# Three output projections one group later in the third stage of a long-convolution kernel, and the ring loads behind them

## The chip, the cores and the metric

The kernel runs on one core of a Trainium2 chip. The metric is the device time of one execution in microseconds. Before the change three runs took 935.6, 933.1 and 936.11 us (median 935.6). One execution was also profiled.

Five engines run side by side, each through its own queue in order: TensorE (PE for its matmuls, PEld for its weight loads), VectorE (DVE), ScalarE (ACT), GpSimd (POOL) and SyncE (SP, which here only starts transfers). ScalarE's queue starts some transfers too.

## The reference, cut to what matters

Eight batches of 6400 tokens with 128 channels, in float32. A causal convolution over the whole length, one filter for each channel, then a gated block:

```
x = irfft(rfft(x, 2*S) * rfft(h, 2*S))[:, :S]        # S = 6400, per channel
gate_pre[t] = sum over k < 5 of conv_w[k] * x[t-4+k]  # five taps, per channel
gate = sigmoid(gate_pre)
out = (gate * (x @ w_val)) @ w_out                    # two 128x128 projections
```

## The kernel before, in words

**The convolution in four stages.** The 6400 tokens are a grid of 100 by 64 (`N1`, `N2`). A first stage (`Forward.half`, table `r1_sb`) transforms along the 100, a second (`s2_mm`, table `m2` from memory) along the 64 for each frequency; its result is multiplied with the filter's spectrum, which the kernel computed at its start and keeps in memory (`hd`). A third stage (`s3_quads`, table `r3_sb`) and a fourth (`Chunk.s4`, table `m4_sb`) transform back. The second stage and the spectrum products run in 13 blocks (`kb`), each with 512 KB of table and 512 KB of spectrum.

**A batch in two parts.** The first part is 16 groups (`for g in range(NS)`, line 663). Group `g` does eight channels of batch b's third stage and eight channels of batch b+1's first stage, and some gated-block work of batch b-1. The second part interleaves the fourth stage of batch b with the second stage of batch b+1. The fourth stage gives the convolution's result in 13 chunks, named by their first column: 60 (four columns) and 0, 5, ..., 55 (five columns each, a tile of 128 channels by 500 tokens). Chunks 10 to 55 of a batch are not finished there: most of their gated block is left to the 16 groups of the next batch (the outputs of 55 and 60 follow in its second part). So in batch 0 no chunk is pending in the groups, and in batch 7 there is no first stage of a next batch.

**A chunk's steps.** `taps` adds the five-tap sum into gate tiles (ScalarE, VectorE, and `add` on GpSimd). `project` is the value projection (two matmuls on TensorE into one PSUM bank), `sigm` the sigmoid on ScalarE, and `gate` multiplies the value in PSUM into the gate tile on VectorE, after which that bank is free. `output` is the output projection (two matmuls into another bank); `store` copies it to SBUF on ScalarE, after which that bank is free, and starts its transfer to memory on SP's queue. Two tables say in which group a chunk takes which step: `VALUE` (line 48) for `project`, `sigm` and `gate`, `OUTPUT` (line 49) for `output`; `store` follows one group after `output` (lines 657 to 661). Within a group the pending chunks come in the order 60, 35, 40, 45, 50, 55, 10, 25, 15, 20, 30, each with all its steps of that group. "Value 30" and "output 20" below are chunk 30's value projection and chunk 20's output projection.

**A group's program.** TensorE: 64 matmul records of the third stage into a pair of PSUM banks, 32 of the first stage into two single banks, then the chunks' projections (four records each). ScalarE: a copy of half of the pair ("keep") and two small copies ("ends"), then, where the group has one, the start of a ring load (`ahead`), then two copies of the first stage's banks, then chunk work. VectorE: two additions that read the pair and set it free ("joins"), then taps and gates of the chunks. GpSimd: the first stage's sums for the group after next (each set free for a load of x on SP's queue), then `add`.

**PSUM.** Two pairs of banks serve the third stage, and four single banks (the pool `ps1`, line 632) everything else: the first stage's two halves, value and output projections. Which single bank a tile gets is fixed when the program is laid out, from the order in which banks come free in the plan; a tile whose bank is still in use waits on the chip for the instruction that frees it.

**The order.** Every instruction is kept in the order in which the program traces it on its engine (`keep_in_program_order`, line 122). Engines wait for each other only where data or a buffer makes them. All instructions therefore carry line 122 in the profile; they are told apart by tile names.

**The ring.** One SBUF tile of seven slots (`ring`) is shared. In the second part slots 0, 1, 2 hold blocks of the table `m2` and slots 3 to 6 spectrum blocks. In the groups the same space holds pending chunks: the gate tiles of chunks 10 to 30 lie in slots 0 to 2 (`held_c`, line 163), their convolution results in slots 2 to 4 (`held_y`, line 164); `store` writes the finished output over that result. As chunks finish, the first blocks of the second part are loaded back in halves of 256 KB, on ScalarE's queue. The table `AHEAD` (line 52) says in which group: `(0, kb, half)` loads a half block of `m2`, which needs the gate tiles there to have been read by `output`; `(1, kb, half)` loads a half block of the spectrum, which needs the stored outputs there to have left for memory.

The lines of a group's pending work:

```
            steps[t] += [c.project]
            steps[t if a in OUTPUT else NS - 1] += [c.sigm, c.gate]
            if a in OUTPUT:
                steps[OUTPUT[a]] += [c.output]
                steps[OUTPUT[a] + 1] += [c.store]
```

Of the kernel before, what the change touches and what calls it, by code (L numbers as in the profile page):

```python
# [45 lines left out]
M2_AT = (14, 19, 24, 27, 29)  # L46
KR = 117
VALUE = {10: 0, 15: 1, 20: 2, 25: 4, 30: 5, 35: 6, 40: 8, 45: 10, 50: 12, 55: 14}
OUTPUT = {10: 2, 15: 3, 20: 4, 25: 6, 30: 7, 35: 8, 40: 9, 45: 11, 50: 13}
ORDER = (60, 0, 35, 40, 45, 50, 55, 5, 10, 25, 15, 20, 30)  # L50
KEEP = {0: 1, 5: 3, 10: 1, 15: 2, 20: 3}
AHEAD = {
    2: (1, 0, 0), 3: (1, 0, 1), 4: (0, 0, 0), 5: (0, 0, 1), 7: (1, 1, 0), 8: (0, 1, 0),
    9: (0, 1, 1), 10: (0, 2, 0), 11: (0, 2, 1), 12: (1, 1, 1), 13: (1, 2, 0), 14: (1, 2, 1),
}


# [77 lines left out]
def longconv_moe(ctx: ExitStack, tc: tile.TileContext, x, h, r1, m2, r3, m4, w64, out):  # L135
# [504 lines left out]
    for b in range(B):  # L640
# [4 lines left out]
        for c in pend:  # L645
# [11 lines left out]
# [5 lines that stand above are left out]
        pend = [c for c in pend if c.ch[0] in (HEAD[0], HEAD[0] - CH)]  # L662
# [143 lines left out]
```

## Time and profile before

| | |
|---|---|
| time of the profiled execution | 933.86 us |
| its span, first to last instruction | 932.0 us |
| mean granted TensorE clock | 0.985 |
| TensorE matmul busy | 855.5 us (92%) |
| VectorE busy | 744.5 us (80%) |
| GpSimd busy | 560.4 us (60%) |
| ScalarE busy | 515.7 us (55%) |
| HBM read and written | 135.90 and 32.77 MB, 181 GB/s |

In the rows below a number ahead is the start in us from the span's first instruction, then the length, engine, line, operation, `out<-in` by tile names, shape and count; neighbours of one kind are merged into one row. In brackets stands how long the engine was idle before the row and which engine's work, on which tile, ended that. Names to know: `r_sb,gy` are the third stage's matmuls, `r_sb,sd` the first stage's, `ring,w_sb` the projections of chunks 10 to 30 and `yl,w_sb` or `gl,w_sb` those of later chunks; `dt<-pt,ring` on VectorE are the joins, `ring<-pt,ring` with 500 columns the gates, `SCALAR_TENSOR_TENSOR` the taps; on ScalarE `ring<-pt` with 512 columns is the keep, `gy<-pt` the first stage's copies, `ring<-pt` with 500 columns a store. Ends of matmuls are modelled, so a busy TensorE need not be one at its peak.

### The profile page before, as it was taken

To read this page: it belongs to the slowest core of one execution; us is meant where nothing else is said; L and a number is where in the kernel's file an instruction comes from. 1 tells how busy PE (TensorE), PEld (TensorE's weight loads), DVE (VectorE), ACT (ScalarE), POOL (GpSimd) and SP (SyncE) were. 2 spreads that over 40 slices of the span, in tenths; PEclk is the share of its full clock that TensorE was granted. 3 is DMA by queue.
4 is the path that set the end of the run, shared out by engine and by line. 5 is a ranking of instruction groups with operands and counts; after the bars stand their busy time and mean duration, and the time that the engine had idled before them with its cause. 6 is when DMAs were issued, how large, how long until landed. Compare 5 with 4: busy or idle time off the path is not lost. (4 is left out here: it accounts for less than half of the span.)

```text
span 932.0 us, 48248 instructions
## 1 busy us (share of the span) xinstructions
PE 855.5 (92%) x21360; PEld 683.5 (73%) x21360; DVE 744.5 (80%) x1057; ACT 515.7 (55%) x1238; POOL 560.4 (60%) x570
## 2 busy tenths in 40 slices
PE   6799668999999999999999999999999989999897
PEld 6699668965699558976689567985689657984563
DVE  5456657888887978888797978888897887978786
ACT  6532452277624874177623875167723785258776
POOL 0046644786477864877477855877558763765333
PEclk9899889999999999999999999999999999999999
DMA  7786647926594456925585465925586364921112
GB/s 241 228 294 225 188 140 238 339 67 185 171 312 154 147 175 204 317 70 172 164 298 180 127 189 171 329 87 167 176 275 223 107 181 159 326 78 48 67 57 99
DMA packets 77847, 171.80 MB, mean 184 GB/s; under 512 B 15246, under 2 KB 28558, under 8 KB 77638
## 3 DMA queue, kind: packets, MB, share of 16 engines
q1 hardware_dynamic: 65542, 146.68, 47.0%
q10 hardware_dynamic: 12096, 22.03, 8.2%
q8 instruction: 168, 2.75, 1.3%
q14 instruction: 41, 0.34, 0.1%
HBM read 135.90 MB, written 32.77 MB: 181 GB/s over the span
## 5 line engine op out<-in xcount | busy, mean ns | idle before, releaser
L122 POOL TENSOR_TENSOR gy<-gy,ring 128x512 f32<-128x512 f32 (+1 forms) x182 | 220.4, 1240 | 103.9 <-DVE ring L122 52.6
L122 PEld LDWEIGHTS pt<-r_sb,gy 64*64 64x64 f32 x8192 | 143.2, 138 | 108.1 <-issue 73.9
L122 PEld LDWEIGHTS pt<-m_sb,dt 128*64 128x64 f32 x4096 | 184.8, 136 | 24.0 <-issue 10.6
L122 DVE TENSOR_TENSOR dt<-pt,ring 128x496 f32<-128x496 f32 x256 | 159.6, 665 | 47.2 <-ACT dt L122 45.9
L122 PE MATMUL pt<-m_sb,dt 128*64 128x100 f32 x4096 | 191.4, 248 | 4.3 <-DVE ring L122 2.9
L122 PE MATMUL pt<-gy,ring 128*64 128x128 f32 x3008 | 187.6, 278 | 8.2 <-PE pt L122 3.1
L122 ACT COPY ring<-pt 128x512 f32<-128x512 f32 (+2 forms) x216 | 128.2, 601 | 116.6 <-PE pt L122 48.8
L122 POOL TENSOR_TENSOR sd<-x 128x256 f32<-128x256 f32 x224 | 179.6, 831 | 17.9 <-issue 13.3
L122 PEld LDWEIGHTS pt<-gy,ring 128*64 128x64 f32 x3008 | 174.7, 135 | 20.3 <-PE pt L122 8.0
L122 PE MATMUL pt<-r_sb,gy 64*64 64x64 f32 x8192 | 162.6, 226 | 19.9 <-issue 14.2
L122 PE MATMUL pt<-r_sb,sd 50*64 50x100 f32 x4608 | 141.0, 260 | 25.7 <-issue 18.6
L122 DVE TENSOR_TENSOR gy<-pt,ring 128x1024 f32<-128x1024 f32 (+1 forms) x99 | 117.0, 1182 | 55.5 <-PE pt L122 53.7
L122 PEld LDWEIGHTS pt<-r_sb,sd 50*64 50x64 f32 x4608 | 119.0, 142 | 31.8 <-issue 21.9
L122 DVE TENSOR_TENSOR ring<-pt,ring 128x1024 f32<-128x1024 f32 (+2 forms) x131 | 134.6, 1027 | 7.0
L122 ACT COPY gy<-pt 128x400 f32<-128x400 f32 x256 | 113.5, 503 | 30.8 <-PE pt L122 24.9
L122 ACT COPY yl<-pt 128x500 f32<-128x500 f32 (+1 forms) x89 | 51.2, 575 | 125.9 <-PE pt L122 125.8
L122 POOL TENSOR_TENSOR gl<-gl,p 128x500 f32<-128x500 f32 (+1 forms) x46 | 54.1, 1177 | 101.9 <-DVE gl L122 50.8
L122 ACT COPY dt<-pt 128x16 f32<-128x16 f32 (+3 forms) x318 | 65.3, 265 | 67.5 <-PE pt L122 67.5
L122 DVE SCALAR_TENSOR_TENSOR gl<-yl,w_sb,gl 128x500 f32<-128x500 f32 (+1 forms) x107 | 94.1, 884 | 3.3 <-ACT gl L122 1.2
L122 PE MATMUL pt<-ring,w_sb 128*64 128x500 f32 x320 | 82.6, 602 | 10.0 <-DVE ring L122 9.2
L122 DVE SCALAR_TENSOR_TENSOR ring<-pt,w_sb,ring 128x500 f32<-128x500 f32 (+3 forms) x94 | 63.2, 672 | 11.8 <-ACT ring L122 7.4
L122 POOL TENSOR_TENSOR gy<-gy,m_sb 128x512 f32<-128x512 f32 x24 | 30.4, 1286 | 65.4 <-DVE m_sb L122 65.4
(59 smaller groups left out, 765.7 us busy)
## 6 DMA issues: line engine op xcount, KB each, us to landing
ring<-m SPq DMA_DIRECT2D x66, 512.0 KB
ring<-hd SPq DMA_DIRECT2D x63, 512.0 KB
x<-xl SPq DMA_DIRECT2D x194, 104.0 KB
ring<-hd ACTq DMA_DIRECT2D x42, 256.0 KB
ring<-m ACTq DMA_DIRECT2D x42, 256.0 KB
out<-ring SPq DMA_DIRECT2D x40, 250.0 KB
out<-yl SPq DMA_DIRECT2D x40, 250.0 KB
x<-xl SPq DMA_DIRECT2D x21, 256.0 KB
```

What stands on the lines that cost most here:

```text
L122: return self._tc.keep_in_program_order(call(*args, **kwargs))
```

## The change

The outputs of chunks 10, 15 and 20 move from groups 2, 3 and 4 to groups 3, 4 and 5, and with them their stores from groups 3, 4 and 5 to 4, 5 and 6. Of the ring loads, the two halves of `m2` block 0 move from groups 4 and 5 to 5 and 6, those of `m2` block 1 from groups 8 and 9 to 7 and 8, and the first half of spectrum block 1 from group 7 to 9. All else, the value projections and every later output among it, stays where it was.

```diff
-OUTPUT = {10: 2, 15: 3, 20: 4, 25: 6, 30: 7, 35: 8, 40: 9, 45: 11, 50: 13}
+OUTPUT = {10: 3, 15: 4, 20: 5, 25: 6, 30: 7, 35: 8, 40: 9, 45: 11, 50: 13}
...
 AHEAD = {
-    2: (1, 0, 0), 3: (1, 0, 1), 4: (0, 0, 0), 5: (0, 0, 1), 7: (1, 1, 0), 8: (0, 1, 0),
-    9: (0, 1, 1), 10: (0, 2, 0), 11: (0, 2, 1), 12: (1, 1, 1), 13: (1, 2, 0), 14: (1, 2, 1),
+    2: (1, 0, 0), 3: (1, 0, 1), 5: (0, 0, 0), 6: (0, 0, 1), 7: (0, 1, 0), 8: (0, 1, 1),
+    9: (1, 1, 0), 10: (0, 2, 0), 11: (0, 2, 1), 12: (1, 1, 1), 13: (1, 2, 0), 14: (1, 2, 1),
 }
```

## The prediction

> **What bounds the kernel now.** I read the page's first part, then busy time by stretch for one of the six like batches (its third stage begins at 301.81), then that batch's order of time on TensorE, VectorE and ScalarE.
>
> ```profile
> span 932.0 us, 48248 instructions
> PE 855.5 (92%) x21360; PEld 683.5 (73%) x21360; DVE 744.5 (80%) x1057; ACT 515.7 (55%) x1238; POOL 560.4 (60%) x570
> ```
>
> ```profile
> 301.81:323.30 21.49, 19.44 (x611) 12.01 (x609) 20.05 (x29) 17.33 (x46) 18.56 (x20) 1.00 0.45 138
> 323.30:353.75 30.45, 28.04 (x911) 18.13 (x909) 24.25 (x36) 23.10 (x64) 17.25 (x20) 1.00 0.57 175
> 353.75:408.29 54.54, 53.22 (x1042) 49.00 (x1040) 46.07 (x59) 19.99 (x41) 36.87 (x34) 1.00 0.66 220
> ```
>
> The stretches are groups 0 to 5, groups 6 to 14, and the rest of the batch; columns are length, then busy PE, PEld, DVE, ACT, POOL. Over the whole, PE is the fullest. In groups 0 to 5, the stretch that the change touches, it is not: DVE works 20.05 of 21.49 us, PE 19.44 of modelled, pipelined time. From group 6 on PE is busy 28.04 of 30.45 and 53.22 of 54.54 us, with DVE at 24.25 and 46.07. So what counts is when TensorE begins group 6 (323.30 here): from there on it runs nearly without a break, and a shift is carried to the end of the batch.
>
> ```profile
> 307.42 1.19 PE L122 MATMUL pt<-r_sb,gy 64*64 64x64 f32 x64
> ...
> 309.61 1.06 PE L122 MATMUL pt<-ring,w_sb 128*64 128x500 f32 x4
> ...
> 311.71 1.06 PE L122 MATMUL pt<-ring,w_sb 128*64 128x500 f32 x4 [1.04 <-DVE ring L122]
> ...
> 312.70 1.19 PE L122 MATMUL pt<-r_sb,gy 64*64 64x64 f32 x64
> ...
> 315.50 1.19 PE L122 MATMUL pt<-r_sb,gy 64*64 64x64 f32 x64
> ...
> 318.20 0.20 PEld L122 LDWEIGHTS pt<-ring,w_sb 128*64 128x64 f32 x4 [0.66 <-ACT gy L122]
> ...
> 319.20 1.19 PE L122 MATMUL pt<-r_sb,gy 64*64 64x64 f32 x64
> ...
> 320.79 0.91 PE L122 MATMUL pt<-r_sb,sd 50*64 50x100 f32 x30 [0.24 <-ACT ring L122]
> ...
> 322.31 1.06 PE L122 MATMUL pt<-ring,w_sb 128*64 128x500 f32 x4 [0.61 <-DVE ring L122]
> ...
> 323.30 1.19 PE L122 MATMUL pt<-r_sb,gy 64*64 64x64 f32 x64
> ...
> 324.31 0.87 PE L122 MATMUL pt<-r_sb,sd 50*64 50x100 f32 x32
> ...
> 326.94 1.19 PE L122 MATMUL pt<-r_sb,gy 64*64 64x64 f32 x64
> ...
> 329.73 1.19 PE L122 MATMUL pt<-r_sb,gy 64*64 64x64 f32 x64
> ```
>
> A group starts at its 64 `r_sb,gy` matmuls. Group 7 (326.94 to 329.73), with one projection and no stall, takes 2.79 us; group 6, with two, 3.64. So a second projection is worth 0.85 us of PE. Group 2 takes 5.28, group 4 3.70, group 5 4.10: the stalls. Their releasers say what is missing. The matmul at 322.31 is chunk 30's value projection; its data have long been there, so what it waits for is a PSUM bank.
>
> ```profile
> 306.94 2.31 DVE L122 SCALAR_TENSOR_TENSOR ring<-ring,w_sb 128x500 f32<-128x500 f32 x2 [1.06 <-POOL ring L122]
> ...
> 309.17 1.24 DVE L122 TENSOR_TENSOR dt<-pt,ring 128x496 f32<-128x496 f32 x2
> ...
> 310.99 0.67 DVE L122 TENSOR_TENSOR ring<-pt,ring 128x500 f32<-128x500 f32 x1
> ...
> 316.03 1.24 DVE L122 TENSOR_TENSOR dt<-pt,ring 128x496 f32<-128x496 f32 x2
> ...
> 319.35 2.31 DVE L122 SCALAR_TENSOR_TENSOR gl<-yl,w_sb,gl 128x500 f32<-128x500 f32 x2
> ...
> 321.59 0.67 DVE L122 TENSOR_TENSOR ring<-pt,ring 128x500 f32<-128x500 f32 x1
> ...
> 323.99 0.67 DVE L122 TENSOR_TENSOR ring<-pt,ring 128x500 f32<-128x500 f32 x1
> ...
> 325.37 1.26 DVE L122 TENSOR_TENSOR dt<-pt,ring 128x496 f32<-128x496 f32 x2 [0.71 <-ACT dt L122]
> ```
>
> DVE starts late at 306.94 (it waited for POOL) and from there has work without a gap worth naming until 324.66 (323.99 + 0.67). Its program is the joins of each group, the taps and the gates, all in fixed order. Gate 15 ends at 311.66 and releases TensorE at 311.71; gate 25 ends at 322.26 and releases it at 322.31. DVE gives the tact in groups 1 to 5.
>
> **The banks.** Single-bank PSUM tiles have four banks (call them W, X, Y, Z), and the plan gives a new tile the one that has been free longest. Before: group 2 takes W, X for its two halves of the first stage, Z for output 10, Y (value 15's) for value 20, which waits for gate 15: the row at 311.71. Group 3: W, X, and Y for output 15. Group 4: W, X, Z for value 25, W again for output 20 (waits for the copy of W: the row at 318.20). Group 5: X, Y (output 15's: waits for its store, the row at 320.79), and Z, value 25's, for value 30, which waits for gate 25. Each row fits.
>
> After, by the same rule: group 2 W, X and Z for value 20, with no wait. Group 3 Y, W, and X for output 10. Group 4 Z, Y, W for value 25, Z again for output 15. Group 5 Y, X, then **output 20 takes W, value 25's bank**, and so waits for gate 25; value 30 comes behind it on Y.
>
> **The change part by part.** It adds and removes no instruction.
>
> Output 10 leaves group 2: the stall there goes, and one projection. Group 3 starts at 309.61 + 0.99 = 310.60 (0.99 is 311.71 to 312.70) instead of 312.70; the joins of group 1 that free its pair of banks end at 309.17 + 1.24 = 310.41. Group 3 then has output 10 in place of output 15: 2.80 and 0.05 for gate 15 (311.66), so group 4 starts at 313.45. That has two projections again: 3.64, to 317.09. Group 5's pair waits for the joins of group 3, which end at 317.27; it starts at 317.30 instead of 319.20. PE is 1.9 us ahead, and DVE, whose order has not changed, is where it was.
>
> Group 5 is where this is given back. Its first-stage half ends at 317.30 + 1.01 + 0.87 = 319.2 (1.01 from 323.30 and 324.31). Output 20 must wait for gate 25, still at 322.26: TensorE stands for 3.1 us, and behind output 20 in its queue stand value 30 and the matmuls of group 6, for which gate 30 and the next joins wait. Then output 20 at 322.31, value 30 at 323.16, group 6 at 324.15 where it was 323.30: **+0.85 us**, as a projection that ran ahead of the DVE chain now runs behind it. Gate 30 (at 323.99 before) waits for value 30 some tenths, and VectorE waits longer for group 6 than its 0.71 us. In one batch DVE itself was held in group 4:
>
> ```profile
> 214.47 2.22 DVE L122 SCALAR_TENSOR_TENSOR gl<-yl,w_sb,gl 128x500 f32<-128x500 f32 x2 [0.90 <-ACT gl L122]
> ...
> 217.32 1.06 PE L122 MATMUL pt<-ring,w_sb 128*64 128x500 f32 x4 [0.42 <-DVE ring L122]
> ```
>
> ScalarE comes earlier after the change, so some 0.7 of the 0.90 goes there and 0.2 us of loss stays. Sum over the six batches: 5 x 0.85 + 0.2 = 4.4 us. Batch 0 has no chunks pending in its groups, and batch 7 no first stage to take banks: nothing for both.
>
> The three stores move with their outputs. On ScalarE's queue store 10 now stands ahead of chunk 25's sigmoid, and store 20 ends group 6, which had none:
>
> ```profile
> 319.65 0.61 ACT L122 ACTIVATE ring<-ring 128x500 f32<-128x500 f32 x1
> ...
> 322.52 0.60 ACT L122 COPY ring<-pt 128x500 f32<-128x500 f32 x1
> ...
> 328.25 0.58 ACT L122 COPY ring<-pt 128x512 f32<-128x512 f32 x1 [0.40 <-PE pt L122]
> ```
>
> ```profile
> 323.87 0.37 SPq L122 DMA_DIRECT2D out<-ring  x1
> ...
> 328.45 0.33 ACTq L122 DMA_DIRECT2D ring<-hd  x1
> ```
>
> Sigmoid 25 ends at 320.26, 1.3 us ahead of gate 25, and its group starts earlier: 0.6 us more is covered. Store 20's 0.60 in group 6 meets 0.40 of ScalarE's idle time before 328.25: at most 0.2 us, which DVE's wait covers; uncovered, 0.2 a batch. The three output transfers go to SP's queue a group later, behind that group's x loads; nothing in the stage needs their landing but the moved spectrum load of block 1, first half. It went out 4.6 us after store 20's transfer (323.87 to 328.45) without holding ScalarE. Two groups later for the load against one for the store leaves more: nothing; if the landing took longer, the load would hold ScalarE's queue, with the first-stage copies behind it. The m2 loads move by one group; they read nothing of stores, and their outputs stand a group earlier on PE. They are needed after group 15: nothing.
>
> **What the 3.1 us do to the clock.** In group 11 of batch 6 TensorE stood once for 1.68 us. By stretch, and in order of time:
>
> ```profile
> 766.31:769.73 3.42, 1.74 (x85) 1.43 (x75) 2.85 (x5) 2.39 (x7) 2.81 (x4) 1.00 0.60 183
> 769.73:773.14 3.41, 3.41 (x64) 1.84 (x65) 1.74 (x3) 0.89 (x2) 1.52 (x2) 0.50 0.35 132
> 131.43:134.85 3.42, 1.68 (x96) 1.54 (x91) 1.34 (x3) 1.46 (x5) 2.08 (x3) 1.00 0.29 81
> 889.19:892.61 3.42, 1.83 (x22) 0.85 (x20) 3.22 (x7) 2.29 (x5) 2.26 (x3) 1.00 0.00 0
> ```
>
> ```profile
> 765.86 1.19 PE L122 MATMUL pt<-r_sb,gy 64*64 64x64 f32 x64
> ...
> 768.88 0.91 PE L122 MATMUL pt<-r_sb,sd 50*64 50x100 f32 x29 [1.68 <-issue]
> ...
> 771.58 1.85 PE L122 MATMUL pt<-r_sb,gy 64*64 64x64 f32 x64
> ```
>
> The column ahead of the last two is the granted clock. A stretch of 3.42 us in which PE was busy 1.74 was followed by one of 3.41 us at 0.50. That group took 5.72 us (765.86 to 771.58): 2.80 + 1.68 + **1.24** for the clock. The last two rows show 1.68 and 1.83 busy without a drop after them, so the limit lies near half a stretch. An idle stretch of 3.1 us leaves at least 1.55 in one of two neighbouring stretches of 3.42 and mostly over 2: I expect the drop in five of six batches, at 1.0 us each (1.24, less where a part of the slow stretch falls into the wait): 5.0 us. Bounds: 0, and 6 x 1.7 (all of 3.41 us at half speed) = 10.2.
>
> [...]
>
> **Sum.** The profiled execution took 933.9 us (span 932.0 and 1.9 around it). 933.9 + 4.4 + 5.0 = **943.3 us**. The median of the runs, 935.6, is 1.7 above the profiled one, inside their spread of 933.1 to 936.1; I leave 943.3 and put the 1.7 into the range.
>
> **The rivals.**
>
> [...]
>
> *Value 30 alone waits for gate 25.* If output 20 gets an early bank and value 30 takes W, output 20 fills part of the wait, value 30 starts at 322.31 as before, group 6 at 323.30: 933.9. For it: value 30 has that wait today. Against: the order in which banks come free.
>
> *Faster: neither waits.* If both take the banks of group 5's own first stage, output 20 runs when the copy of the first has ended, at about 320.0, value 30 at 320.8, group 6 at 321.8, 1.5 us earlier. VectorE then decides: its next joins can move from 325.37 to 324.66, 0.7 us. So 0.7 to 1.5 a batch, 1.1 x 6 = 6.6: 927.3. It decides for a gain from the point where value 30 no longer stands behind 322.26. For it: the stall of 1.04 in group 2 does go. Against: gate 25's bank is free ahead of those copies in today's order, as value 30 shows by taking it.
>
> *Slower still:* the clock falls in all six for the full stretch: 933.9 + 4.4 + 10.2 = 948.5.
>
> **How the numbers follow.** Forecast 0.48 (own range 940 to 947), clock holds 0.17, value 30 alone 0.13, neither 0.17, slower still 0.05. About 0.3% (2.8 us) is what a measurement can tell from no change. Faster by more: 0.17 and 0.02 of the unchanged case, 0.19. Within: 0.11 of the unchanged case and 0.04 of the case with the clock held, 0.15. Slower: the rest, 0.66. The range reaches from 930 (most of the faster case left out) to 948.5.
>
> **What would show it.** Right: group 2 at 2.8 us with no wait on DVE; in group 5 the output of chunk 20 with a wait of about 3 us on "DVE ring", and value 30 directly behind it; group 6's first matmul some 22.3 us after the stage's first, where it was 21.49; granted clock 0.50 for 3.4 us near group 6. Wrong: a group 5 without that wait (bank rule), group 6 at 20.0 to 21.5, or a DVE gap before gate 25.

## The result, and the profile after

The kernel after takes 944.55 us (median; 940.35 to 949.96), the kernel before, beside it, 934.35 (931.2 to 936.11). The ratio is **1.0111, 95% interval [1.0074, 1.0148]**: slower by 10.2 us between the medians, where 9.4 was forecast. The profiled execution took 945.33 us, with a granted clock of 0.972 (before 0.985).

The page's first part after the change:

```profile
span 943.5 us, 48238 instructions
PE 863.1 (91%) x21360; PEld 689.7 (73%) x21360; DVE 744.4 (79%) x1057; ACT 515.4 (55%) x1238; POOL 559.5 (59%) x570
```

The span is 11.5 us longer. TensorE has the same 21360 matmuls, yet is busy 7.6 us more (855.5 to 863.1); the rows with a granted clock of 0.50 below show why. The other engines' busy time has hardly moved.

TensorE's order of time in the batch that the prediction showed; its third stage now begins at 302.70 (before 301.81):

```profile
302.70 1.19 PE L122 MATMUL pt<-r_sb,gy 64*64 64x64 f32 x64
...
308.30 1.19 PE L122 MATMUL pt<-r_sb,gy 64*64 64x64 f32 x64
309.66 0.92 PE L122 MATMUL pt<-r_sb,sd 50*64 50x100 f32 x32 [0.17 <-POOL sd L122]
...
311.50 1.19 PE L122 MATMUL pt<-r_sb,gy 64*64 64x64 f32 x64
...
314.54 1.19 PE L122 MATMUL pt<-r_sb,gy 64*64 64x64 f32 x64
...
318.34 1.19 PE L122 MATMUL pt<-r_sb,gy 64*64 64x64 f32 x64
319.35 0.87 PE L122 MATMUL pt<-r_sb,sd 50*64 50x100 f32 x32
323.19 2.41 PE L122 MATMUL pt<-ring,w_sb 128*64 128x500 f32 x8 [2.97 <-DVE ring L122]
325.53 1.99 PE L122 MATMUL pt<-r_sb,gy 64*64 64x64 f32 x64
...
330.19 1.19 PE L122 MATMUL pt<-r_sb,gy 64*64 64x64 f32 x64
```

The rows of 64 `r_sb,gy` are the starts of groups 0, 2, 3, 4, 5, 6 and 7. Group 2, which took 5.28, takes 3.20 us. In group 5 the eight records at 323.19 are output 20 and value 30 in one row: ahead of them TensorE stands for 2.97 us, waiting for VectorE. (In batch 1 it stands there for 1.99 us, in batches 3 to 6 for 2.49 to 3.08.) Group 7 begins 330.19 - 302.70 = 27.49 us after the stage's start, where it began at 326.94 - 301.81 = 25.13.

VectorE's order of time there:

```profile
322.48 0.67 DVE L122 TENSOR_TENSOR ring<-pt,ring 128x500 f32<-128x500 f32 x1
...
325.71 0.68 DVE L122 TENSOR_TENSOR ring<-pt,ring 128x500 f32<-128x500 f32 x1 [0.77 <-PE pt L122]
328.40 1.26 DVE L122 TENSOR_TENSOR dt<-pt,ring 128x496 f32<-128x496 f32 x2 [2.01 <-ACT dt L122]
```

The first row is gate 25: it ends at 323.15, and TensorE goes on at 323.19. It starts 322.48 - 302.70 = 19.78 us after the stage's start, as before (321.59 - 301.81 = 19.78). Gate 30 now waits 0.77 us for value 30, and the next joins 2.01 us, where it was 0.71.

The clock fell to 0.50 for stretches of 3.41 or 3.42 us. The first two rows here and the last two are neighbours, just before and just after the clock fell, in the batch above and in the sixth like batch; the rest are the slow stretches of the other four. The column ahead of the last two is the granted clock.

```profile
321.03:324.44 3.41, 1.25 (x6) 0.49 (x8) 3.37 (x6) 1.14 (x3) 2.80 (x3) 1.00 0.41 115
324.44:327.86 3.42, 3.42 (x84) 2.33 (x84) 1.19 (x2) 0.23 (x1) 2.62 (x3) 0.50 0.72 227
215.22:218.63 3.41, 3.41 (x29) 1.08 (x28) 1.78 (x4) 0.00 (x0) 2.15 (x4) 0.50 0.77 250
433.67:437.08 3.41, 3.41 (x44) 1.26 (x44) 1.86 (x3) 0.00 (x0) 2.14 (x4) 0.50 0.67 229
542.90:546.31 3.41, 3.41 (x36) 1.25 (x36) 1.88 (x4) 0.00 (x0) 2.14 (x4) 0.50 0.61 234
652.12:655.53 3.41, 3.41 (x70) 1.84 (x69) 1.51 (x3) 0.00 (x0) 2.44 (x3) 0.50 0.61 195
757.94:761.35 3.41, 0.88 (x4) 0.34 (x6) 3.37 (x5) 1.40 (x4) 3.16 (x4) 1.00 0.46 148
761.35:764.76 3.41, 3.41 (x66) 1.83 (x66) 1.55 (x3) 0.00 (x0) 2.39 (x3) 0.50 0.65 202
```

The clock fell behind the wait in **six batches of six**. Elsewhere in those batches it fell once in either kernel: before, in group 11 of batch 6 (0.50 from 769.73 to 773.14), and after, in group 11 of batch 2 (0.50 from 344.93 to 348.34).

**Where the 11.5 us lie.** Three parts of the span, from the starts of the groups; the middle one is batches 1 to 6, split at group 7. They alone have the moved outputs beside a first stage that takes banks: batch 0 has only moved ring loads, and batch 7 the moved outputs but no first stage.

| | before | after | difference |
|---|---|---|---|
| start of batch 1 (the kernel's head and batch 0) | 196.16 | 194.35 | -1.8 |
| six times from a batch's start to its group 7 | 151.35 | 165.20 | +13.85 |
| six times from group 7 to the next batch | 487.80 | 487.41 | -0.4 |
| batch 7 and the end | 96.74 | 96.59 | -0.15 |

All of the loss arises ahead of group 7, and what arises there is still there at the batch's end. The -1.8 lies in the head and batch 0, where the change moves nothing but the starts of five ring loads. Over the kernels below that have just these loads, that start spreads from 194.1 to 203.0 us.

### The profile page after: what moved, and what is told of

The parts are those of the page before. It is cut to its first block, busy times and chain, and to the rows that moved or that the text cites. A ratio compares the mean times of both kernels' runs of the same rounds, so it can differ in the third digit from the quotient of the medians.

```text
span 943.5 us, 48238 instructions
## 1 busy us (share of the span) xinstructions
PE 863.1 (91%) x21360; PEld 689.7 (73%) x21360; DVE 744.4 (79%) x1057; ACT 515.4 (55%) x1238; POOL 559.5 (59%) x570
## 4 chain that ended last, share of the span: by engine, by line
PE 69%; DVE 9%; issue 7%; POOL 5%; ACT 4%; DMA 4%; SPq 1%; POOLq 0%; DVEq 0%; ACTq 0%
PE pt L122 69%; DVE ring L122 4%; DVE dt L122 3%; ACT ring L122 2%; DVE gl L122 2%; POOL ring L122 2%; DMA ring<-m 1%; POOL gl L122 1%; DMA m_sb<-xl 1%; POOL sd L122 1%; SPq L122 1%; ACT gy L122 1%; DMA x<-xl 1%; DVE gy L122 1%; DMA x<-hl 0%
## 5 line engine op out<-in xcount | busy, mean ns | idle before, releaser
L122 PEld LDWEIGHTS pt<-r_sb,gy 64*64 64x64 f32 x8192 | 148.3, 142 | 113.8 <-issue 68.7
L122 ACT COPY ring<-pt 128x500 f32<-128x500 f32 (+2 forms) x216 | 128.6, 600 | 137.9 <-issue 63.2
L122 PE MATMUL pt<-r_sb,gy 64*64 64x64 f32 x8192 | 167.4, 231 | 21.9 <-issue 15.5
L122 PE MATMUL pt<-ring,w_sb 128*64 128x500 f32 x320 | 86.7, 639 | 15.7 <-DVE ring L122 15.6
L122 DVE SCALAR_TENSOR_TENSOR gl<-yl,w_sb,gl 128x500 f32<-128x500 f32 (+1 forms) x107 | 90.4, 850 | 2.4 <-POOL gl L122 0.4
L122 POOL TENSOR_TENSOR gy<-gy,m_sb 128x512 f32<-128x512 f32 x24 | 30.4, 1286 | 60.8 <-DVE m_sb L122 60.8
```

Of the source, the lines that this page charges most:

```text
L122: return self._tc.keep_in_program_order(call(*args, **kwargs))
```

## The experiments

**The theory**: output 20 takes value 25's bank, stands behind gate 25, and this costs twice, by the order on TensorE (0.86 us a batch) and by the clock that falls behind the idle time. **Rivals**: the moved loads hold a queue; the later outputs and stores cost by themselves, whatever bank they have; the clock's part is nothing, or is all of it.

A table for reading along: where group 6 begins in batch 2 (us from the stage's start), the sum of the six stretches ahead of group 7 and of the six behind it in the profiled execution, the clock's falls in group 5 or 6 of the six batches, and the ratio to the kernel before, timed on the same chip.

| kernel | group 6, batch 2 | six to group 7 | six behind it | falls | ratio, interval |
|---|---|---|---|---|---|
| before | 21.49 | 151.35 | 487.80 | 0 | 1 |
| after | 22.84 | 165.20 | 487.41 | 6 | 1.0111 [1.0074, 1.0148] |
| loads alone | 21.49 | 150.77 | 486.84 | 0 | 1.0009 [0.9982, 1.0035] |
| after, first stage three times | 22.34 | 157.42 | 485.43 | 1 | 1.0066 [1.0032, 1.0099] |
| after, first stage twice | 22.33 | 160.74 | 488.37 | 3 | 1.0130 [1.0092, 1.0167] |
| after, gate 25 first | 20.72 | 146.42 | 494.54 | 0 | 0.9986 [0.9959, 1.0012] |
| before, gate 25 first | 20.34 | 144.87 | 489.96 | 0 | 0.9982 [0.9958, 1.0006] |
| output 20 alone later | 21.50 | 151.71 | 489.42 | 0 | 1.0014 [0.9991, 1.0037] |
| outputs 10 and 15 later | 23.23 | 170.24 | 483.62 | 6 | 1.0169 [1.0139, 1.0198] |
| 10 later, gate 25 first | 19.99 | 142.23 | 493.40 | 0 | 1.0002 [0.9979, 1.0025] |

### The moved loads alone

The kernel after, with the outputs where they were:

```diff
-OUTPUT = {10: 3, 15: 4, 20: 5, 25: 6, 30: 7, 35: 8, 40: 9, 45: 11, 50: 13}
+OUTPUT = {10: 2, 15: 3, 20: 4, 25: 6, 30: 7, 35: 8, 40: 9, 45: 11, 50: 13}
```

> The ring loads in their new groups, the outputs of chunks 10, 15 and 20 in their old ones. Bank theory (the loss is output 20's wait for gate 25's bank and the clock that falls behind it): no wait of 3 us in group 5, group 6 starts 21.5 us after the stage's first matmul as before, no clock drop there, the time of the kernel before within 0.3%. Rival (the moved transfers cost something, by holding ScalarE's queue or by crowding x loads and instruction loads): a good part of the 1.1% stays, 0.3% or more, seen as longer groups 7 to 9 or a longer batch 0.

It took 932.88 us beside 933.17. Group 7 begins where it began before: 25.10 to 25.14 us after the stage's start in batches 2 to 6 (before 25.10 to 25.12), and in batch 1 at 25.16, without the hold that made it 25.79 before. The moved loads cost nothing that can be measured (by the interval at most 0.35%); this rival falls.

### The wait filled with work: first stage three times, and twice

The kernel after; in group 5 of the batches with pending chunks TensorE computes the first stage's halves three times over, into the same banks. The gate on which output 20 waits comes no sooner, but TensorE has work until then.

```diff
-        def half(self, pt=None):
+        def half(self, pt=None, again=0):
...
-            for m in range(XG):
+            for m in [m for _ in range(again + 1) for m in range(XG)]:
...
+        pend_now = bool(pend)
...
-                f = fx.half([single(), single()])
+                f = fx.half([single(), single()], 2 if pend_now and g == 5 else 0)
```

> The changed kernel with one addition: in group 5 of batches 1 to 6 the first-stage matmuls are computed three times over into the same two banks, so that TensorE works some 1.7 us of the 3 us in which it stood, and still waits for gate 25 afterwards. Bank and clock theory: the wait before output 20 shrinks to about 1.3 us, the granted clock stays at 1.00 in the third stages of batches 1 to 6, group 7 starts some 26 us after the stage's first matmul in place of 27.5, and the time falls by 6 x 1.5 = 9 us although work was added: about 1.003 of before, the 0.85 us per batch of the wait being left. Rival (the clock is a bystander, the wait alone costs 2.4 us per batch): the time of the changed kernel or more, 1.011 of before.

Its TensorE in batch 2 (from 304.01) and in batch 1 (from 196.25):

```profile
319.73 1.23 PE L122 MATMUL pt<-r_sb,gy 64*64 64x64 f32 x64
...
324.52 1.90 PE L122 MATMUL pt<-ring,w_sb 128*64 128x500 f32 x8
326.35 1.19 PE L122 MATMUL pt<-r_sb,gy 64*64 64x64 f32 x64
...
329.98 1.19 PE L122 MATMUL pt<-r_sb,gy 64*64 64x64 f32 x64
```

```profile
216.75 3.36 PE L122 MATMUL pt<-ring,w_sb 128*64 128x500 f32 x8 [1.70 <-DVE ring L122]
```

Batch 2 gives the prediction's step as it was worked out, without the clock: group 6 at 326.35 - 304.01 = 22.34 (forecast 22.34), group 7 at 25.97. So it is in five batches: group 7 is 0.83 to 0.88 behind before, 0.86 in the mean. TensorE still stood somewhere in group 5 of each batch, for 1.1 to 1.7 us; in batch 1 the clock fell behind its 1.70 us (0.50 from 217.04 to 220.45), and group 7 began at 27.59. In the kernel after, where the clock fell in all six, group 7 begins at 27.49 to 27.57, 27.53 in the mean: **one fall is worth 27.53 - 25.97 = 1.56 us**. Within this one execution it is 27.59 - 25.97 = 1.62.

By these figures the order alone costs 5 x 0.86 in batches 2 to 6 and 25.97 - 25.79 = 0.18 in batch 1, 4.5 us, and the one fall 1.6: 6.1. By the ratio, 1.0066, the time was 6.2 us longer, twice what was expected: the expectation took six falls off the loss and so came out below the 0.85 us a batch that it left standing itself, and one fall remained. At group 7 it was 7.8 us less than in the kernel after. By the ratios the two differ by 4.2 us, with intervals of some 3 us to either side for each, so the timed runs alone don't show that the filled wait is faster; the starts of the groups show it.

With two passes in place of three (`1 if pend_now and g == 5 else 0`) a wait of about 2 us stays:

> The changed kernel with group 5's first-stage matmuls of batches 1 to 6 computed twice over (not three times) into the same banks: about 2.1 us of standing is left before output 20. If the clock falls when a stretch of 3.41 us has about 1.7 us or more of idle, it falls in about half of the six batches, group 7 starts at 26.0 us in the others and near 27.3 us in those: 1.006 to 1.010 of before. Rival (the clock falls only for an idle time of 3 us in one piece, which the changed kernel just has): no drop in the six batches, group 7 at 26.0 us in all.

It lost the clock in three batches of six. The wait and the stretch of the clock in batch 2 (no fall), then in batch 4 (fall):

```profile
332.11 1.90 PE L122 MATMUL pt<-ring,w_sb 128*64 128x500 f32 x8 [2.27 <-DVE ring L122]
...
546.07 3.35 PE L122 MATMUL pt<-ring,w_sb 128*64 128x500 f32 x8 [1.73 <-DVE ring L122]
```

```profile
327.91:331.32 3.41, 1.92 (x95) 1.73 (x85) 3.24 (x4) 2.72 (x9) 3.41 (x5) 1.00 0.34 97
331.32:334.74 3.42, 2.63 (x60) 1.29 (x64) 3.16 (x6) 0.46 (x1) 2.15 (x3) 1.00 0.62 177
542.95:546.36 3.41, 1.68 (x67) 1.39 (x60) 3.24 (x5) 2.74 (x8) 3.41 (x5) 1.00 0.39 107
546.36:549.78 3.42, 3.42 (x24) 0.92 (x24) 1.71 (x4) 0.00 (x0) 2.15 (x3) 0.50 0.76 235
```

The longer wait, of 2.27 us, did not cost the clock, and the shorter, of 1.73, did. The boundary at 331.32 cuts the longer one into 1.49 and 0.79 of idle time; the shorter lies whole in one stretch. The rows are laid at whole multiples of 3.413 us from the fall at 546.36 (331.32 is 215.04 ahead of it, 63 x 3.413). In the profiled executions of the kernels before and after, the changes of the clock, 13 and 23 of them, all lie whole multiples of 3.413 us apart; the six falls behind the wait, for one, are 109.22 or 109.23 apart, 32 x 3.413. What fits these rows is how much idle time falls into one such stretch. In group 5 the clock fell behind 1.70 us of idle time (three passes, batch 1, 213.62 to 217.04), 1.73 (two passes, batch 4), 1.80 (outputs 10 and 15 alone later, batch 2, 322.18 to 325.60) and 1.99 to 2.53 (the kernel after, all six); it held behind 1.49 (two passes, batch 2) and 1.66 (outputs 10 and 15 alone later, batch 2, 318.77 to 322.18).

Group 7 began at 25.97 in the three batches without a fall and at 27.58 to 27.67 in the others: between the kernel with three passes and the kernel after, as the theory has it. **The measured ratio does not lie between**: 1.0130 where 1.006 to 1.010 was expected. Its interval reaches down to 1.0092, so six runs (940.89 to 950.65 us) don't exclude a time between either. In the profiled execution, the slowest of the six, the excess is in the head and batch 0 (batch 1 starts at 203.04; from 94.9 to 166.0 us the page's granted clock, in tenths, reads 6, 8, 8), in which nothing differs from the kernel after. Whether this kernel does worse there as a rule was not settled.

### The wait taken away: gate 25 first

In the kernel after, and in a second one with the tables of before, chunk 25's value, sigmoid and gate stand first in their group, ahead of the taps of a later chunk (`WAIT` is 25):

```diff
-            steps[t] += [c.project]
-            steps[t if a in OUTPUT else NS - 1] += [c.sigm, c.gate]
+            if a == WAIT:
+                steps[t][:0] = [c.project, c.sigm, c.gate]
+            else:
+                steps[t] += [c.project]
+                steps[t if a in OUTPUT else NS - 1] += [c.sigm, c.gate]
```

> The changed kernel, but in group 4 chunk 25's value projection, sigmoid and gate come ahead of chunk 35's taps, so that gate 25 ends some 2.3 us earlier in VectorE's order, at about 18.1 us after the stage's first matmul in place of 20.5. Bank theory: the long wait in group 5 goes (at most 1.5 us is left, ahead of the first stage's second bank), group 6 starts at about 20.7 us, VectorE's wait before the joins of group 6 closes (0.7 us), no clock drop: 0.995 of before, 0.984 of the changed kernel. Rival (the moved transfers, or the order of outputs itself, cost it): the time stays near 1.011 of before.

> The kernel before, with the same order in group 4: chunk 25's value projection, sigmoid and gate ahead of chunk 35's taps. Theory (value 30 stands behind gate 25 in the kernel before, and VectorE's fixed order sets that gate): the stalls of 0.24 and 0.61 us in group 5 go, group 6 starts at about 20.3 us in place of 21.5, VectorE's idle 0.7 us before group 6's joins closes, and 0.7 to 1.2 us per batch are won: 928 to 930, 0.992 to 0.996 of before. Rival (the batch is paced elsewhere, so that group 6's earlier start is given back at the next stall): 0.998 to 1.002.

Gate 25 on VectorE in the kernel after with this edit, batch 2 (from 302.41), then groups 5 and 6 and the start of 7 on TensorE:

```profile
319.75 0.66 DVE L122 TENSOR_TENSOR ring<-pt,ring 128x500 f32<-128x500 f32 x1
```

```profile
317.94 1.20 PE L122 MATMUL pt<-r_sb,gy 64*64 64x64 f32 x64
...
320.46 0.91 PE L122 MATMUL pt<-r_sb,sd 50*64 50x100 f32 x30 [1.18 <-DVE ring L122]
321.31 1.90 PE L122 MATMUL pt<-ring,w_sb 128*64 128x500 f32 x8
323.13 1.19 PE L122 MATMUL pt<-r_sb,gy 64*64 64x64 f32 x64
...
326.77 1.19 PE L122 MATMUL pt<-r_sb,gy 64*64 64x64 f32 x64
```

Gate 25 ends 319.75 + 0.66 - 302.41 = 18.00 us after the stage's start, where it was 20.45 (323.15 - 302.70); group 5 begins at 15.53, as in the kernel after (15.64). The wait shrinks to 1.18 us (the second half of the first stage has gate 25's bank here), the clock holds (0.985 in the mean, as before), and the loss is gone: 0.9986 with the outputs, stores and loads as late as in the kernel after, beside 0.9982 for the kernel before with the same edit. **It is the wait that costs, not the later outputs.** That rival falls.

Neither kernel gained what it was expected to (0.995, and 0.992 to 0.996). Group 7 begins 4.9 and 6.5 us earlier in sum than before, but the stretches behind it are 6.7 and 2.2 us longer. This is taken up at the end of the section.

### Which output is later: 20 alone, 10 and 15 alone

The loads are those of the kernel after.

```diff
-OUTPUT = {10: 3, 15: 4, 20: 5, 25: 6, 30: 7, 35: 8, 40: 9, 45: 11, 50: 13}
+OUTPUT = {10: 2, 15: 3, 20: 5, 25: 6, 30: 7, 35: 8, 40: 9, 45: 11, 50: 13}
```

> Output 20 alone in group 5 (10 and 15 in groups 2 and 3 as before), the ring loads as in the changed kernel. Bank theory: here the rule gives output 20 the bank of output 15, free when store 15 has ended in group 4 (about 19.0 us after the stage's first matmul), and value 30 takes gate 25's bank as before; output 20 fills a wait that was there, group 6 starts at 21.5 us, no clock drop: the time of the kernel before within 0.3%. Rival (output 20 standing ahead of value 30 in group 5 is itself what costs, whatever its bank): group 6 at 22.3 us or later, 1.005 to 1.011.

and `{10: 3, 15: 4, 20: 4, ...}` in its place:

> Outputs 10 and 15 in groups 3 and 4 as in the changed kernel, output 20 left in group 4, the ring loads as in the changed kernel. Bank theory: now it is the second bank of group 5's first stage that is gate 25's; TensorE stands some 3 us ahead of it until 20.5 us, then does the first stage and value 30: group 6 at about 22.7 us, a clock drop in most batches, 1.009 to 1.013 of before, though output 20 was not moved. Rival (output 20's move is what costs): the time of the kernel before, 1.000.

TensorE with output 20 alone later, from group 5 of batch 2 (its stage begins at 305.42):

```profile
322.25 1.19 PE L122 MATMUL pt<-r_sb,gy 64*64 64x64 f32 x64
...
324.67 1.06 PE L122 MATMUL pt<-ring,w_sb 128*64 128x500 f32 x4
325.93 1.06 PE L122 MATMUL pt<-ring,w_sb 128*64 128x500 f32 x4 [0.20 <-DVE ring L122]
326.92 1.19 PE L122 MATMUL pt<-r_sb,gy 64*64 64x64 f32 x64
```

With outputs 10 and 15 alone later, from 302.86:

```profile
319.17 1.19 PE L122 MATMUL pt<-r_sb,gy 64*64 64x64 f32 x64
...
323.37 0.91 PE L122 MATMUL pt<-r_sb,sd 50*64 50x100 f32 x30 [2.85 <-DVE ring L122]
324.89 1.27 PE L122 MATMUL pt<-ring,w_sb 128*64 128x500 f32 x4 [0.60 <-ACT gy L122]
326.09 1.99 PE L122 MATMUL pt<-r_sb,gy 64*64 64x64 f32 x64
```

Output 20 in group 5, as late as in the kernel after, costs nothing when outputs 10 and 15 have not moved: it then gets output 15's bank and runs at once (324.67), and value 30 waits 0.20 us for gate 25's bank, as value 30 did before. And moving 10 and 15 without 20 is the **worst of all**, 1.0169, where 1.009 to 1.013 was expected: now the second half of the first stage has value 25's bank, so that this half, its copy, and behind them value 30 all stand behind gate 25 (2.85 us), and a further 0.60 for the copy; the clock falls in six batches of six (in batch 2 it is 0.50 from 325.60 to 329.01; 0.974 in the mean). The order of time follows the banks; which projection is later decides only which tile gets the bad one.

### No wait for gate 25, and where a lead goes

Output 10 alone later, with gate 25 first; with the loads of the kernel after:

```diff
-OUTPUT = {10: 3, 15: 4, 20: 5, 25: 6, 30: 7, 35: 8, 40: 9, 45: 11, 50: 13}
+OUTPUT = {10: 3, 15: 3, 20: 4, 25: 6, 30: 7, 35: 8, 40: 9, 45: 11, 50: 13}
```

> Output 10 alone in group 3, 15 and 20 in groups 3 and 4 as before, chunk 25's value projection, sigmoid and gate ahead of chunk 35's taps in group 4, the ring loads as in the changed kernel. Theory: group 2's stall on gate 15 goes (2.8 us in place of 5.3) and nothing stands behind gate 25 for long (it ends near 18.1 us): group 6 at 20.0 to 20.5 us, VectorE paces up to group 6's joins, no clock drop; 0.995 to 0.999 of before, as good as the two kernels with gate 25 first. Rival (TensorE's instruction waits in groups 8 to 14 give the lead back whole): 1.000.

Nothing in groups 5 and 6 waits for gate 25 now, which the prediction's fast rival had too, though by another placing: here output 20 stands in group 4, and the gate itself comes earlier. Group 6 of batch 2 begins at 19.99, 1.5 us ahead of before, as that rival had it, and group 7 9.1 us ahead in sum. The time did not move: 1.0002. TensorE's waits by what released them, sum, times and longest ("issue": nothing awaited that the profile shows), first the kernel before, then this one:

```profile
PE pt L122 <- issue: 32.9, 32, 2.8
PE pt L122 <- DVE ring L122: 14.2, 23, 1.4
...
PE pt L122 <- DVE gl L122: 4.8, 4, 1.5
...
PE pt L122 <- ACT gy L122: 2.7, 8, 1.0
```

```profile
PE pt L122 <- issue: 30.3, 27, 2.9
PE pt L122 <- ACT gy L122: 10.0, 18, 1.5
...
PE pt L122 <- DVE gl L122: 6.3, 10, 1.5
...
PE pt L122 <- DVE ring L122: 4.6, 11, 1.4
```

The waits for the early chunks' gates fell by 9.6 us, and 7.3 came back as waits for ScalarE's copies of the first stage and 1.5 for later chunks' gates, mostly in groups 7 and 8, which take 20.7 and 27.2 us in the sum of six batches, where before it was 17.4 and 23.4. The stretches behind group 7 are 5.6 us longer. By these waits, TensorE arrives sooner where ScalarE and VectorE are no sooner. Of the profiled execution's 2.9 us gain (span 929.1) the timed runs show nothing.

In the kernel after with gate 25 first the lead went another way: its waits in which nothing was awaited rose.

```profile
PE pt L122 <- issue: 37.7, 34, 3.1
PE pt L122 <- DVE ring L122: 11.4, 18, 1.4
```

Whether these 4.8 us more belong to the earlier start or to this one execution was not settled. No variant tried is faster than the kernel before by more than its interval; the nearest is the kernel before with gate 25 first, 0.9982 [0.9958, 1.0006].

## Why the prediction was right, and what in it was not

**Forecast 943.3, measured 944.55 (profiled: 945.33).** Its mechanism is the one that the runs show; one term of its sum was too small, and others, that it did not have, made up for part of it.

- *What bounds: group 6's start counts, and a shift is carried to the end.* Right for the delay: 13.85 us at group 7, 13.5 at the batches' ends. Not right as a general rule: the leads of 4.9, 6.5 and 9.1 us came back by 6.7, 2.2 and 5.6 us behind group 7. The fast rival, worked out at 927.3 by carrying its 1.1 us a batch to the end, would have been wrong by this, as the last experiment shows; and other delays (6.1 and 18.9 us) were made up by 2.4 and 4.2. Of these, differences near 2 us are no more than one execution scatters: with output 20 alone later, where group 7 starts as before within 0.4 us in sum, the stretches behind it are 1.6 longer.
- *The banks.* Right. Output 20 waits for gate 25, value 30 comes directly behind it. The traces name no banks, but the plans in which the kernels before and after are laid out do, and in them every bank of groups 2 to 5 of batch 2 is as the prediction has it. The placing of the rival "value 30 alone" turned up with output 20 alone later, and group 6 began where the rival had it (21.50, worked out at 21.49). The placing of "neither" turned up in no experiment; its start of group 6 did (19.99), in the last one.
- *Groups 3, 4 and 5 earlier.* Forecast from the stage's start: 8.79, 11.64, 15.49. Measured in batch 2: 8.80, 11.84, 15.64.
- *The wait.* Forecast 3.1 us, measured 2.97 in batch 2, with gate 25 at the same 19.78; 1.99 to 3.08 over the six batches.
- *+0.85 a batch and +0.2 in the one that was held, 4.4 us.* Right: 0.86 and 0.18, 4.5 us, where TensorE was kept busy.
- *Stores, sigmoid, loads at nothing.* Right for the loads by themselves (1.0009). For the stores it rests on the two kernels with gate 25 first: 0.9986 with the later stores, 0.9982 without. The sigmoid held nothing: gate 25 starts at the same 19.78.
- *The clock: five batches of six at 1.0 us, 5.0 us.* **This term was mis-sized: six of six at 1.56 us, 9.4 us.** That the clock would fall, behind idle time near half a stretch, was right (it fell behind 1.70 us and more of 3.41 in group 5), and the other case, in which it holds (933.9 + 4.4 = 938.3, at a chance of 0.17), did not come. The price had been read from a single group, 1.24 us, and that group ends at 771.58, while its slow stretch runs to 773.14. The rest of the loss lies in the next group, whose first 64 matmuls the prediction's last row shows at 1.85 us in place of 1.19. It ends here:

```profile
775.04 1.18 PE L122 MATMUL pt<-r_sb,gy 64*64 64x64 f32 x62
```

That group, 12, took 775.04 - 771.58 = 3.46 us in place of 2.80, 0.66 more, so the fall was worth up to 1.24 + 0.66 = 1.90 there. The 1.24 was then lowered further, for the part of the slow stretch that would fall into the wait. None did: the fall came at the end of the stretch in which TensorE stood, and by then the wait was over (in batch 2 it ended at 323.19, and the slow row begins at 324.44; in the other batches too the wait ended first). TensorE is busy for all of the 3.41 us in each of the six slow rows, at a granted clock of 0.50, so by estimate the price lies near half of that, 1.7. The bound, 10.2, held.
- *The sum.* 4.5 + 9.4 = 13.9 us is what batches 1 to 6 show at group 7 (13.85). That is a division of the loss and no second proof of it, as the 1.56 is taken from the same starts; the falls with two passes, 27.58 to 27.67 against 25.97 in one execution, give 1.61 to 1.70 by themselves. The profiled execution is only 11.5 longer, since its head and batch 0 were 1.8 us shorter, with the 0.4 and 0.15 of the table. Had the prediction sized the clock as it is, it would have come to 933.9 + 4.4 + 9.4 = 947.7, above the median that was measured and inside the runs' spread (940.35 to 949.96). So the closeness of 943.3 is in part luck.
- *What would show it.* Each sign named came: the wait of about 3 us on "DVE ring", the 0.50 row near group 6, group 2 without its wait on VectorE (it took 3.20, not 2.8: its first stage, at 309.66, waits for GpSimd's sums). Group 6's 22.3 is seen where the clock holds; with the fall it is 22.84 to 23.69.

## What to carry to other kernels

A PSUM tile's bank follows here from the order in which banks come free in the program, so moving one instruction can hand a bank to another tile and set a wait in front of it (output 20 waited 2.97 us for value 25's bank, and ran at once on output 15's); write down the banks of the next few tiles before and after, and see which instruction frees the one that the moved tile gets. The wait on TensorE cost twice here, 0.86 us a batch by its order and 1.56 by the clock at 0.50 behind it, where 1.70 us or more of idle time in group 5 fell into one stretch of 3.41: price such a wait with its order and with the clock, and take the clock's price from all of the work that runs in the slow stretch. A lead that one stage gains need not reach the end: the leads of 4.9, 6.5 and 9.1 us at group 7 came back by 6.7, 2.2 and 5.6 behind it.

## What the runs showed of the hardware that was not expected

- The clock fell behind stretches that were idle for about half or more: in group 5 behind 1.70 us of idle time (1.72 busy of 3.42), 1.73 and more, and not behind 1.66. Elsewhere these records, whose matmul ends are modelled, show no sharp limit: the clock fell behind 1.68 us (before, group 11 of batch 6), 1.76 (after, group 11 of batch 2, 341.51 to 344.93) and 1.55 (after, 24.07 to 27.48), and held behind 1.59 and 1.74 (the prediction's rows at 889.19 and 131.43) and 2.06 (two passes, 48.02 to 51.43).
- A wait's length alone did not decide: with two passes, 2.27 us cut by a boundary kept the clock, and 1.73 within one stretch lost it.
- TensorE stands for some 30 to 38 us of a profiled execution with nothing awaited that the profile shows: 32.9 us in 32 waits before, 30.4 in 34 after, 37.7 in 34 with gate 25 first, 30.3 in 27 with output 10 later and gate 25 first, each wait 3.1 us at most. Why was not settled. They lie at other places from kernel to kernel, and in sum they are longer than the whole loss sought here.
- Batch 0 and the head, in which the edits move nothing but the starts of five ring loads, ended between 194.1 and 203.0 us. A difference below this spread, seen in one profiled execution, says nothing until it is located in the batch that was changed.
